# Shifted steps, later x loads and a longer estimate of a PSUM hold in a planned conv + ELU-MLP kernel

## Chip, cores and metric

One core of one Trainium2 chip. The metric is the device time of one execution in microseconds (us), lower is better. All runs named here are of one core and of the fast state; where a ratio to the kernel before is given, the two ran in turns on the same chip, and it is the mean time of one kernel's fast runs over the mean of the other's fast runs of the same rounds. It is therefore not quite the ratio of the medians that are quoted beside it. The experiments ran in four batches, on different chips (the record names 6, 13, 6 and 5), so absolute times of different batches are compared with less certainty.

## The reference

```python
def _attn_ref(x, weight):                       # x (8, 4096, 192), weight (8, 7)
    w = softmax(weight, axis=-1)                # cut: written out in numpy
    x_pad = np.concatenate([np.zeros((B, 6, D)), x], axis=1)
    idx = np.arange(S)[:, None] + np.arange(7)[None, :]
    x_unf = x_pad[:, idx, :].reshape(B, S, K, H, 24)
    return np.einsum('hk,bskhg->bshg', w, x_unf).reshape(B, S, D)

def _moe_ref(x, w_in, w_out):                   # x (32768, 192), w_in (192, 2048)
    h = x @ w_in
    g = np.where(h > 0.0, h, np.exp(np.minimum(h, 0.0)) - 1.0)
    return g @ w_out
```

A causal convolution of seven taps, one filter for each of 8 heads, is followed by a two-layer MLP with ELU between the layers.

## The kernel before

The 32768 rows go through in 32 blocks ("supers") of 1024. For each super TensorE computes

- four conv units (`"c"`, banded matrix times x),
- 16 pairs of h units (`"h"`: 128 of the 2048 hidden columns times 512 rows, one unit `r` for each half of the rows), three matmuls of 512 columns each,
- four output accumulators (`"o"` matmuls into a bank `"a"`), each open for eight pairs.

K is cut to 64, so that two matmuls run beside each other in the upper and the lower half of the array ("row half" 0 and 1; in the trace of this kernel a matmul of 64 x 512 and one of 64 x 192 both start at 209.06 us). An h unit goes through four engines: TensorE writes it to a PSUM bank, ScalarE (ACT) takes `E = exp(h)`, GpSimd (POOL) clamps E to 0..1, VectorE (DVE) computes `max(h, E - 1)` from E and the bank. Only then is the bank free. There are eight banks for h units, conv units and accumulators together, and a planner in Python fixes the whole order of TensorE, and which bank each unit takes, before the kernel is built:

```python
O_AT = (12, 15)              # pair at which the first and the second accumulator open
CONV_AT = (14, 18, 22, 25)   # pairs at which the conv units of a super two ahead run
HELD = {"h": 2500.0, "c": 1300.0, "a": 1400.0}   # ns from last matmul to a free bank, estimated
X_AT = ((1, 1, 1), (0, 1, 0))  # (conv unit, supers ahead, half): x load issued behind it

def take_bank(what):
    if what not in bank_of:
        b = min(range(NBANK), key=lambda b: freed[b])   # the bank expected free first
        bank_of[what], prior[what] = b, occupant[b]
        occupant[b], freed[b] = what, float("inf")

def h_items(n, r):
    def issue(j):
        take_bank(("h", n, r))
        plan.append((clock[r], ("h", n, r, j)))
        freed[bank_of["h", n, r]] = clock[r] + MM_H + HELD["h"] if j == 2 else float("inf")
# ... c_items, o_items and emit (which merges the two row halves by their clocks) are cut

# POOL: x loads stand between the clamps, issued by POOL (queue q0, software_dynamic, on the page)
for i, (n, u) in enumerate(units):
    # ... w_out load at pair W_OUT_AT = 5, zeroing of the pad rows: cut
    for to_load in x_before.get(i, ()):
        load_x(*to_load)
    W(s_exp, i + 1)
    g.tensor_scalar(out=E[:, i % NE, :], in0=E[:, i % NE, :],
                    scalar1=1.0, scalar2=0.0, op0=ALU.min, op1=ALU.max).then_inc(s_clp)

# TensorE: the first matmul into a bank waits for the last reader of its old user
def wait_bank(what):
    was = prior[what]
    # ...
    if was[0] == "h":   W(s_tt, tt_count(*was[1:]))       # DVE done
    elif was[0] == "c": conv_read(W, was[1])              # ACT done
    else:               W(s_oev[was[2]], was[1] + 1)      # ACT done
```

Below, "pair 5" means the pair with n mod 16 = 5 within a super (conv steps 14, 18, 22 and 25 are pairs 14, 2, 6 and 9), and "period" the time of one super.

## Time and profile before

| what | value | from |
|---|---|---|
| time | 754.69 us, median of 3 runs: 749.99, 754.69, 754.84 | the runs |
| span of the profiled run | 746.8 us (its time: 748.59) | page |
| TensorE, ACT, POOL, DVE busy | 99, 90, 89, 86% | page, part 1 |
| one period, measured | 22.21 us | trace: first h matmul of pair 32 to that of pair 464, over 27 |
| one period, as planned | 21.75 us | worked out in the prediction |

The lines behind these are in the prediction. One more view of the kernel before is needed later: the waits between 60 and 640 us, where the periods repeat. The columns are engine and line, who ended the wait, us in total, times, longest.

```profile
DVE gT L535 <- POOL E L455: 59.4, 150, 1.1
PEld H L589 <- DVE gT L535: 4.4, 26, 0.4
```

In 26 periods the weight load of conv unit 1 (line 589) waited for DVE, once each. This list sees only stretches in which the whole row PEld (TensorE's weight loads) is idle; a late matmul of one row half beside a busy other half isn't in it. That is why the prediction compares each start with the plan.

### The profile page before, as it was taken

To read this page: it belongs to the slowest core of one execution; us is meant where nothing else is said; L and a number is where in the kernel's file an instruction comes from. 1 tells how busy PE (TensorE), PEld (TensorE's weight loads), DVE (VectorE), ACT (ScalarE), POOL (GpSimd) and SP (SyncE) were. 2 spreads that over 40 slices of the span, in tenths; PEclk is the share of its full clock that TensorE was granted. 3 is DMA by queue.
4 is the path that set the end of the run, shared out by engine and by line. 5 is a ranking of instruction groups with operands and counts; after the bars stand their busy time and mean duration, and the time that the engine had idled before them with its cause. 6 is when DMAs were issued, how large, how long until landed. Compare 5 with 4: busy or idle time off the path is not lost.

```text
span 746.8 us, 27602 instructions
## 1 busy us (share of the span) xinstructions
PE 738.9 (99%) x11862; PEld 670.0 (90%) x11862; DVE 642.9 (86%) x1034; ACT 669.3 (90%) x1281; POOL 668.2 (89%) x1110
## 2 busy tenths in 40 slices
PE   8999999999999999999999999999999999999998
PEld 4379999999999999999999999999999999999997
DVE  2588898888998888889888989888899889898994
ACT  1689999999999999999999999999999999999993
POOL 3899999999999999999999999999999999998893
PEclk9999999999999999999999999999999999999999
DMA  5963455453445454445355345446344444453312
GB/s 99 135 87 70 77 86 80 76 84 71 89 74 89 66 83 75 90 70 94 60 86 90 72 72 92 68 87 84 70 81 84 83 72 83 71 94 69 56 46 66
DMA packets 135499, 59.32 MB, mean 79 GB/s; under 512 B 101680, under 2 KB 134576, under 8 KB 135376
## 3 DMA queue, kind: packets, MB, share of 16 engines
q0 software_dynamic: 44992, 17.67, 23.0%
q1 hardware_dynamic: 90112, 39.68, 22.9%
q8 instruction: 93, 1.52, 0.8%
q14 instruction: 30, 0.25, 0.1%
q10 hardware_dynamic: 272, 0.20, 0.1%
HBM read 34.80 MB, written 25.45 MB: 81 GB/s over the span
## 4 chain that ended last, share of the span: by engine, by line
PE 94%; DMA 3%; POOL 2%; DVE 1%; ACT 0%; issue 0%; SPq 0%
PE H L633 52%; PE H L610 37%; PE H L589 4%; POOL E L455 2%; DMA w_out<-in_moe_w_out_dram 1%; PE H L572 1%; DMA conv_band<-wprb 1%; POOL xg L405 1%; DMA wq<-in_weight_dram 0%; DMA Tk<-conv_band 0%; DVE gT L535 0%; ACT E L482 0%; ACT csb L478 0%; DVE osb L546 0%; DVE wprb L517 0%
## 5 line engine op out<-in xcount | busy, mean ns | idle before, releaser
L535 DVE SCALAR_TENSOR_TENSOR gT<-E,H 128x512 f16<-128x512 f32 x1024 | 637.2, 683 | 79.4 <-POOL E L455 78.7
L633 PE MATMUL H<-w_out,gT 64*128 64x192 f16 x8192 | 692.7, 243 | 1.6 <-DMA w_out<-in_moe_w_out_dram 1.4
L610 PE MATMUL H<-att,w_in 64*128 64x512 bf16 x3072 | 692.7, 376 | 0.5 <-DVE gT L535 0.3
L633 PEld LDWEIGHTS H<-w_out,gT 64*128 64x128 f16 x8192 | 622.5, 94 | 40.2 <-DVE gT L535 1.9
L455 POOL TENSOR_SCALAR E<-E 128x512 f32<-128x512 f32 x1024 | 604.6, 612 | 53.6 <-ACT E L482 39.3
L482 ACT ACTIVATE E<-H 128x512 f32<-128x512 f32 x1024 | 589.7, 603 | 52.9 <-PE H L610 26.4
L610 PEld LDWEIGHTS H<-att,w_in 64*128 64x128 bf16 x3072 | 273.8, 93 | 10.7 <-issue 5.1
L589 PE MATMUL H<-xg,Tm 64*112 64x240 bf16 x496 | 95.2, 272 | 0.1
L478 ACT ACTIVATE csb<-H 112x480 bf16<-112x480 f32 x126 | 70.9, 564 | 11.1 <-PE H L589 11.1
L491 ACT ACTIVATE osb<-H 128x384 f32<-128x384 f32 x127 | 62.7, 494 | 7.7 <-PE H L633 7.7
L405 POOL DMA_DIRECT2D xg<-in_x_dram x65 | 59.3, 912 | 6.0 <-DVE csb L525 5.8
L589 PEld LDWEIGHTS H<-xg,Tm 64*112 64x112 bf16 x496 | 53.9, 125 | 5.8 <-DVE gT L535 5.1
L572 PE MATMUL H<-zw 128*128 128x512 bf16 x86 | 24.6, 433 | 1.5 <-DVE zw L502 1.5
L572 PEld LDWEIGHTS H<-zw 128*128 128x128 bf16 x86 | 8.3, 109 | 15.3 <-issue 6.7
L525 DVE CAST csb<-H 112x480 bf16<-112x480 f32 x2 | 1.3, 658 | 10.4 <-PE H L589 10.4
L546 DVE COPY osb<-H 128x384 f32<-128x384 f32 x1 | 0.6, 557 | 7.9 <-PE H L633 7.9
L437 POOL DMA_DIRECT2D w_in<-w_in x1 | 0.7, 680 | 5.4 <-DMA w_in<-in_moe_w_in_dram 5.4
L423 POOL DMA_DIRECT2D w_in<-in_moe_w_in_dram x6 | 3.5, 599 | 0.9 <-DMA att<-csb 0.9
L589 PEld LDWEIGHTS H<-xg,Tk 64*112 64x112 bf16 (+1 forms) x16 | 2.6, 296 | 1.5 <-DMA Tk<-conv_band 1.5
L589 PE MATMUL H<-xg,Tk 64*112 64x240 bf16 (+1 forms) x16 | 2.9, 382 | 1.0 <-DMA Tk<-conv_band 1.0
L526 DVE COPY Tm<-Tk 118x896 bf16<-118x896 bf16 x1 | 2.2, 2190 | 0.0
L504 DVE TENSOR_REDUCE wmx<-wq 128x8 f32<-128x56 f32 x1 | 0.2, 210 | 2.2 <-DMA wq<-in_weight_dram 2.2
(17 smaller groups left out, 7.9 us busy)
## 6 DMA issues: line engine op xcount, KB each, us to landing
out_dram<-osb SPq DMA_DIRECT2D x127, 192.0 KB, 3.2
xg<-in_x_dram POOLq DMA_DIRECT2D x62, 240.0 KB, 5.0
w_in<-in_moe_w_in_dram POOLq DMA_DIRECT2D x6, 128.0 KB, 5.2
w_out<-in_moe_w_out_dram POOLq DMA_DIRECT2D x1, 768.0 KB, 8.6
att<-csb SPq DMA_TRANSPOSE x32, 3.8
xg<-in_x_dram POOLq DMA_DIRECT2D x2, 192.0 KB, 4.0
w_in<-w_in POOLq DMA_DIRECT2D x1, 384.0 KB, 4.4
w_in<-w_in SPq DMA_DIRECT2D x1, 384.0 KB, 6.6
```

The costliest lines, as they stand in the source:

```text
L405: g.dma_start(xg[0:rows, b, 2 * w0 + gr : 2 * w1 : 2, :], src).then_inc(s_x[b][gr], 16)
L423: g.dma_start(w_in[0:HP, j, c0:c1], bass.AP(tensor=moe_w_in.tensor, offset=8 * j * FF + c0, ap=[[CPH * FF, HEADS], [FF, 8], [1, c1 - c0]], ...
L455: g.tensor_scalar(out=E[:, i % NE, :], in0=E[:, i % NE, :], scalar1=1.0, scalar2=0.0, op0=ALU.min, op1=ALU.max,).then_inc(s_clp)
L478: a.activation(*conv_evac(W, m), ACT.Copy).then_inc(s_ce)
L482: a.activation(E[:, i % NE, :], H[:, bank_of[item], :], ACT.Exp).then_inc(s_exp)
L491: a.activation(osb[:, k % 2, g, :, :].rearrange("p k d -> p (k d)"), acc_of(k, g)[:, 0 : 2 * D], ACT.Copy,).then_inc(s_oev[g])
L526: v.tensor_copy(Tm[0:KW, :, :].rearrange("p h t -> p t h"), Tk[0:KW, :, :]).then_inc(s_tm)
L535: v.scalar_tensor_tensor(out=gT[:, s % NG3, q, u, :], in0=E[:, i % NE, :], scalar=1.0, in1=H[:, bank_of["h", n, u], :], op0=ALU.subtract, ...
L572: pe.matmul(H[:, bank_of[item[:2]], :], zw[:, 0:P], zw[:, 0:GS], start=True, stop=True)
L589: ins = pe.matmul(H[0:CW, bank_of["c", m], 256 * q : 256 * q + UC], Tm[rows, h, :] if s else Tk[rows, :, h], xg[rows, s % NXB, :, CPH * h ...
L610: ins = pe.matmul(H[:, bank_of[item[:3]], :], w_in[HP * r : HP * (r + 1), j, FC * q : FC * (q + 1)], att[HP * r : HP * (r + 1), s % 2, j, ...
L633: ins = pe.matmul(acc_of(k, g)[:, D * kb : D * (kb + 1)], gT[HP * rt : HP * (rt + 1), t % NG3, q, g, t0 : t0 + P], w_out[HP * rt : HP * (r ...
```

## The change

The intent, in the words given with it: the planned order is shifted, with conv units and x loads at other steps, the second accumulator one pair later, and banks picked by a longer estimate of an h unit's hold. The core of the diff:

```diff
-O_AT = (12, 15)
-CONV_AT = (14, 18, 22, 25)
+O_AT = (12, 16)
+CONV_AT = (14, 18, 23, 25)
-HELD = {"h": 2500.0, "c": 1300.0, "a": 1400.0}
+HELD = {"h": 2900.0, "c": 1300.0, "a": 1400.0}
-X_AT = ((1, 1, 1), (0, 1, 0))
+X_AT = ((2, 1, 1), (1, 1, 0))
+DVE_LAG = 1000.0
+E_DVE = ()
+X_WHOLE = False
+X_OFF = 0
```

The rest (cut) rewrites the loops of DVE and SyncE so that they follow a planned order too, and adds switches that are off here: evictions by DVE (`E_DVE` empty), one load for both halves (`X_WHOLE` false).

More of the change, by code (lines that the diff above doesn't have):

```diff
@@ L227, in bass_lightweight_conv__then__act_elu_kernel @@
     turn_at = {}
-    for item in pe_order:
+    dve_order, evacs, unit_at_conv = [], [], {}
+    for at, item in sorted(plan, key=lambda p: p[0]):
         if item[0] == "h" and item[3] == 2:
+            dve_order.append((at + DVE_LAG, item[:3]))
             unit_at[item[1:3]] = len(units)
@@ L234, in bass_lightweight_conv__then__act_elu_kernel @@
             act_order.append(item[:2])
+            unit_at_conv[item[1]] = at
         elif item[0] == "o" and item[-1]:
@@ L237, in bass_lightweight_conv__then__act_elu_kernel @@
             if turn_at[item[1:3]] == visits[item[1:3]]:
-                act_order.append(("e",) + item[1:3])
+                what = ("e",) + item[1:3]
+                if item[2] in E_DVE or item[1:3] == (NK - 1, 1):
+                    dve_order.append((at + AHEAD, what))
+                else:
+                    act_order.append(what)
+                evacs.append((at, what))
+    dve_order = [what for _, what in sorted(dve_order, key=lambda p: p[0])]
     assert len(units) == 2 * NP
@@ L250, in bass_lightweight_conv__then__act_elu_kernel @@
             if s + ahead < NS:
-                x_before.setdefault(before, []).append((s + ahead, gr))
+                x_before.setdefault(before + X_OFF, []).append((s + ahead, gr))
     x_before.setdefault(X_EARLY, []).append((2, 1))
@@ L298, in bass_lightweight_conv__then__act_elu_kernel @@
         s_cd = sema("s_cd")
-        s_od = sema("s_od")
         s_wdp = sema("s_wdp")
@@ L311, in bass_lightweight_conv__then__act_elu_kernel @@
         s_att = [sema(f"s_att{i}") for i in range(2)]
+        s_od = sema("s_od")
         s_cswap = sema("s_cswap")
@@ L330, in bass_lightweight_conv__then__act_elu_kernel, with x_whole @@
         WCOLS = ((0, P * QA), (P * QA, FF))
+        def x_whole(s):
+            return X_WHOLE and 2 < s < NS - 1
         x_need, z_need, z_count = {}, {}, 0
@@ L336, in bass_lightweight_conv__then__act_elu_kernel @@
             for g in range(2):
-                x_count[s % NXB][g] += 16 + 16 * ((s, g) in ((0, 0), (NS - 1, 1)))
+                if g == 0 or not x_whole(s):
+                    x_count[s % NXB][g] += 16 + 16 * ((s, g) in ((0, 0), (NS - 1, 1)))
                 x_need[s, g] = x_count[s % NXB][g]
@@ L372, in acc_of, with evacuated_by, out_evac @@
             return H[:, bank_of["a", k, g], :]
+        def evacuated_by(W, k, g):
+            on_dve = [item[1:] for item in dve_order if item[0] == "e"]
+            if (k, g) in on_dve:
+                W(s_od, on_dve.index((k, g)) + 1)
+            else:
+                W(s_oev[g], [a for a in act_order if a[0] == "e" and a[2] == g].index(("e", k, g)) + 1)
+        def out_evac(W, k, g):
+            W(s_out[k % 2], 32 * (k // 2))
+            W(s_fin[g], k + 1)
+            return (
+                osb[:, k % 2, g, :, :].rearrange("p k d -> p (k d)"),
+                acc_of(k, g)[:, 0 : 2 * D],
+            )
         def transpose(eng, W, s):
@@ L397, in load_x @@
                     ).then_inc(s_x[0][0], 16)
+                if x_whole(s):
+                    if gr == 0:
+                        src = bass.AP(
+                            tensor=x_flat.tensor,
+                            offset=(s * SUP - PAD) * D,
+                            ap=[[D, P], [CW * D, NWIN], [GS * D, 2], [1, D]],
+                        )
+                        g.dma_start(
+                            xg[:, b, :, :].rearrange("p (w g) d -> p w g d", g=2), src
+                        ).then_inc(s_x[b][0], 16)
+                    return
                 def windows(w0, w1, rows):
@@ L485, in _scalar @@
                 else:
-                    _, k, g = item
-                    if (k, g) == (NK - 1, 1):
-                        continue
-                    W(s_fin[g], k + 1)
-                    W(s_out[k % 2], 32 * (k // 2))
-                    a.activation(
-                        osb[:, k % 2, g, :, :].rearrange("p k d -> p (k d)"),
-                        acc_of(k, g)[:, 0 : 2 * D],
-                        ACT.Copy,
-                    ).then_inc(s_oev[g])
-            W(s_od, 1)
+                    a.activation(*out_evac(W, *item[1:]), ACT.Copy).then_inc(s_oev[item[2]])
+            evacuated_by(W, NK - 1, 1)
             out_group(a, NK - 1, 1)
@@ L528, in _vector @@
             ).then_inc(s_tm)
-            for i, (n, u) in enumerate(units):
+            for item in dve_order:
+                if item[0] == "e":
+                    v.tensor_copy(*out_evac(W, *item[1:])).then_inc(s_od)
+                    continue
+                _, n, u = item
+                i = unit_at[n, u]
                 s, q = divmod(n, NQ)
@@ L538, in _vector @@
                     scalar=1.0,
-                    in1=H[:, bank_of["h", n, u], :],
+                    in1=H[:, bank_of[item], :],
                     op0=ALU.subtract,
@@ L542, in _vector @@
                 ).then_inc(s_tt)
-            b = (NK - 1) % 2
-            W(s_fin[1], NK)
-            W(s_out[b], 32 * (NS - 1))
-            v.tensor_copy(
-                osb[:, b, 1, :, :].rearrange("p k d -> p (k d)"),
-                acc_of(NK - 1, 1)[:, 0 : 2 * D],
-            ).then_inc(s_od)
         @block.tensor
@@ L563, in wait_bank @@
                 else:
-                    W(s_oev[was[2]], was[1] + 1)
+                    evacuated_by(W, *was[1:])
             turns, done = {0: 0, 1: 0}, {}
@@ L671, in _sync @@
             ).then_inc(s_band, 16)
-            for item in act_order:
+            sync_work = []
+            for m in range(CU - 1, CU * NS, CU):
+                sync_work.append((unit_at_conv[m], ("c", m)))
+            sync_work += [(at, item) for at, item in evacs]
+            for _, item in sorted(sync_work):
                 if item[0] == "c":
-                    s, u = divmod(item[1], CU)
-                    if u == CU - 1:
-                        transpose(sy, W, s)
+                    transpose(sy, W, item[1] // CU)
                     if item[1] == CU - 1:
@@ L681, in _sync @@
                         sy.dma_start(w_in[HP:P, :, c0:c1], w_in[0:HP, :, c0:c1]).then_inc(s_wd, 16)
-                elif item[0] == "e" and item[1:] != (NK - 1, 1):
-                    W(s_oev[item[2]], item[1] + 1)
+                elif item[1:] != (NK - 1, 1):
+                    evacuated_by(W, *item[1:])
                     out_group(sy, *item[1:])
```

## The prediction

> **What bounds the kernel now.** I read the page first: its busy shares, its chain, its costliest groups.
>
> ```profile
> PE 738.9 (99%) x11862; PEld 670.0 (90%) x11862; DVE 642.9 (86%) x1034; ACT 669.3 (90%) x1281; POOL 668.2 (89%) x1110
> PE 94%; DMA 3%; POOL 2%; DVE 1%; ACT 0%; issue 0%; SPq 0%
> L535 DVE SCALAR_TENSOR_TENSOR gT<-E,H 128x512 f16<-128x512 f32 x1024 | 637.2, 683 | 79.4 <-POOL E L455 78.7
> L405 POOL DMA_DIRECT2D xg<-in_x_dram x65 | 59.3, 912 | 6.0 <-DVE csb L525 5.8
> ```
>
> TensorE sets the end, but "99% busy" cannot tell whether it runs at full pace: two 64-row halves of the array work beside each other, and one half hides the other's gap. So I worked out what a period must cost. A period is one block of 1024 rows, 16 "pairs" of h units; the trace spaces matmuls of one half 216 ns apart (512 columns) and 82.5 ns (192), and the plan has 102.5 for 240. One half does 48 x 216 + 128 x 82.5 + 8 x 102.5 ns = **21.75 us**. Then I looked for the real period in the order in time of POOL (first of two answers) and DVE (second), near the middle of the run.
>
> ```profile
> 199.87 1.33 POOL L455 TENSOR_SCALAR E<-E 128x512 f32<-128x512 f32 x2
> 201.14 0.89 POOL L405 DMA_DIRECT2D xg<-in_x_dram  x1
> 202.07 4.70 POOL L455 TENSOR_SCALAR E<-E 128x512 f32<-128x512 f32 x8
> 206.71 0.90 POOL L405 DMA_DIRECT2D xg<-in_x_dram  x1
> ...
> 223.33 0.90 POOL L405 DMA_DIRECT2D xg<-in_x_dram  x1
> ```
>
> ```profile
> 202.73 4.89 DVE L535 SCALAR_TENSOR_TENSOR gT<-E,H 128x512 f16<-128x512 f32 x8 [0.81 <-POOL E L455]
> 208.31 4.92 DVE L535 SCALAR_TENSOR_TENSOR gT<-E,H 128x512 f16<-128x512 f32 x8 [0.69 <-POOL E L455]
> ```
>
> The same x load is issued at 201.14 and at 223.33, so the period is **22.2 us**: 0.45 us over the plan, 32 times. The reader is to see how each POOL issue of 0.9 us leaves DVE idle 0.7 to 0.8 us and then with a queue of eight units. Third, the order in time around two late TensorE starts.
>
> ```profile
> 204.67 0.12 PEld L589 LDWEIGHTS H<-xg,Tm 64*112 64x112 bf16 x1 [0.15 <-DVE gT L535]
> 204.67 0.31 PE L589 MATMUL H<-xg,Tm 64*112 64x240 bf16 x1
> ...
> 209.06 0.39 PE L610 MATMUL H<-att,w_in 64*128 64x512 bf16 x1
> ```
>
> The conv matmul at 204.67 takes the PSUM bank of an h unit that DVE frees as the third of the queue begun at 202.73 (202.73 + 2 x 0.60 + 0.68 = 204.61). The h matmul at 209.06 takes a bank freed by the first unit of the queue begun at 208.31 (ends 208.99). Both start 0.06 us after the release, and every period repeats them. By comparing each start with the planned time, the first late start is worth 0.20 us on its half (and 0.04 as its next weight load is late too), the second 0.21 us on the other half, and a third, conv unit 2, 0.04. The chain calls all this PE, since the other half was busy meanwhile.
>
> [...]
>
> **The change part by part.** No arithmetic is added or removed: the counts of instructions per engine are the same in both built programs, X_WHOLE is off, E_DVE empty, and DVE's order is unchanged. Only the order moves. The rule for each hand-over of a bank: wait = hold + 0.06 us - distance, with the hold from the old user's last matmul start to the end of its last reader, and the distance from that start to the planned start of the new user. From the trace, per place in the period: h holds are 2.42 to 2.75 us where POOL is undisturbed and 2.77 to 3.10 in the six to eight units behind an x issue; a conv unit holds 1.15 us. The planner of the kernel, followed item by item, gives the distances.
>
> Before: x issues fall at pairs 14 and 2 of the period. Conv unit 1 (pair 2) takes the bank of the r = 0 unit of pair 15, distance 2.83, hold 2.99: wait 0.22. The h unit of pair 5 takes that of pair 2, distance 2.83, hold 2.99: wait 0.22. The trace has 0.20 and 0.21, so the rule works.
>
> 1. *x loads one conv unit later* (X_AT): issues move from pairs 14 and 2 to pairs 2 and 7. This clears the long holds at pairs 14 to 1 (they fall to about 2.45 to 2.6), so conv unit 1 has 2.83 against 2.5: its wait goes, -0.24. In exchange pairs 7 to 9 get holds of about 3.0. The data still come in time: issue to landing is 5.0 us (6.4 at most in the view of that line), the conv that needs them is 7 pairs, 9.5 us, later.
> 2. *HELD h 2.5 to 2.9*: the planner now gives the h units of pairs 5 to 7 banks with a distance of 3.49 us, against holds of up to 3.03: the second wait goes, -0.21. It shifts the squeeze to conv banks and accumulators.
> 3. *Conv unit 2 at pair 7, second accumulator at 16*: conv unit 2 takes the bank of pair 4's unit, distance 2.83 against 2.77 + 0.06: about 0, as tight as can be. The second accumulator's odd turn (pair 8) takes conv unit 2's bank, distance 1.09 to 1.15 against 1.15 + 0.06: **a new wait of 0.06 to 0.11**, plus 0.05 where the next half waits for its turn. The pair-10 unit takes that of pair 7: 3.15 against 3.03 + 0.06, just clear.
>
> Sum per period: 0.45 - 0.24 - 0.21 - 0.04 + 0.10 + 0.05 (rounding up for the tight ones) = 0.11 to 0.16 left; I take 0.16, a gain of 0.29. Steady periods: about 29, as the first two and the end differ: 29 x 0.29 = 8.4 us. Against it: about 0.4 us at the start, where the longer estimate makes early units wait for conv banks (most of it hidden, since TensorE then waits for w_out anyway), and 0.3 us at the tail, where the plan itself ends 697.75 instead of 697.42 us. Net **-7.7 us, an estimate**.
>
> **The rivals.** (a) *The wait only moves*: the backlog behind an x issue now meets conv unit 2, pair 10 and the odd accumulator with 0.0 to 0.1 us to spare. For it: h holds of r = 0 vary by 0.1 between neighbouring places. Against it: most distances grew from 2.83 to 3.49. If two of the three lose 0.15 more, the gain is 0.29 - 0.2 = 0.1 a period, some 3 us: about 751. (b) *All waits vanish*: 0.40 a period, 12 us, about 742 from the median. (c) *The bound is elsewhere* (ACT, POOL, DVE at 86 to 90%): then nothing moves, 754; against it, each of the three has idle time behind TensorE and the two waits are seen. (d) *Later x loads come too late* for conv or for the zeroing on POOL (7 times): some us slower; the landing of 6.4 us against 8 to 9.5 speaks against it.
>
> **Range and chances.** Before ran at 749.99, 754.69 and 754.84, and 748.59 under the profile: two levels 5 us apart. A POOL issue 0.08 us longer would do that (2 x 0.08 x 30 = 4.8 us, an estimate from the two waits with no slack), but this is not shown; it may as well lie in the start. The change should take off 7.7 from either level: 747 or 742. I put the middle at **745.5 us**, range 739 to 751.5. To be faster by over 2% of the 753 mean it would have to save 15 us, more than all steady waits together (0.45 x 32 = 14.4): 0.05. Slower by over 2%: 0.02. Within 2%: 0.93.
>
> **What would show each step right or wrong.** In the changed trace: the spacing of the x issues from period to period (21.9 us right; 22.1 or more wrong); conv unit 1 and pair 5 without a wait for DVE; TensorE's repeated wait now before the second accumulator, released by ACT's conv eviction, near 0.1 us; DVE's idle of 0.7 to 0.8 us behind POOL at pairs 2 and 7. The prediction fails if a hand-over with under 0.1 us to spare waits in each period, if POOL's issues last longer beside other transfers, or if the start differs.

## The result, and the profile after

The first comparison, four runs each: the changed kernel 740.92 us (740.60 to 742.02), the kernel before 752.34 us (749.52 to 754.84), ratio 0.9852 with a 95% interval of 0.9804 to 0.9900. By the 2% rule that is "same"; the interval lies clear of 1. Compared again with 6 and 27 runs (below) the ratio was 0.9866.

The page of the changed kernel, with the lines that answer to those of before:

```profile
span 738.9 us, 27599 instructions
PE 730.6 (99%) x11859; PEld 686.2 (93%) x11862; DVE 639.3 (87%) x1034; ACT 674.9 (91%) x1281; POOL 670.1 (91%) x1110
PE 94%; DMA 3%; POOL 2%; DVE 0%; ACT 0%; issue 0%; DVEq 0%; SPq 0%
L575 DVE SCALAR_TENSOR_TENSOR gT<-E,H 128x512 f16<-128x512 f32 x1024 | 633.6, 683 | 73.8 <-POOL E L499 72.2
L449 POOL DMA_DIRECT2D xg<-in_x_dram x65 | 59.3, 912 | 6.5 <-DVE csb L560 6.3
```

The busy shares and the chain look as before: the work is the same and TensorE was "99% busy" in both. Only the weight-load row moves, from 670 to 686 us at the same number of loads, whose lengths add up to 1130 and 1132 us, so fewer of them lie beside each other; I did not follow that further. The page alone would not tell what was gained.

The order in time does. First POOL, then DVE, in the changed kernel near 200 us (start, length, what):

```profile
205.19 0.89 POOL L449 DMA_DIRECT2D xg<-in_x_dram  x1
206.11 5.89 POOL L499 TENSOR_SCALAR E<-E 128x512 f32<-128x512 f32 x10
211.95 0.90 POOL L449 DMA_DIRECT2D xg<-in_x_dram  x1
212.89 4.86 POOL L499 TENSOR_SCALAR E<-E 128x512 f32<-128x512 f32 x8
...
227.06 0.90 POOL L449 DMA_DIRECT2D xg<-in_x_dram  x1
```

```profile
206.77 6.07 DVE L575 SCALAR_TENSOR_TENSOR gT<-E,H 128x512 f16<-128x512 f32 x10 [0.69 <-POOL E L499]
213.55 4.92 DVE L575 SCALAR_TENSOR_TENSOR gT<-E,H 128x512 f16<-128x512 f32 x8 [0.71 <-POOL E L499]
```

The same x load comes at 205.19 and 227.06: a period of **21.87 us** here, 21.89 over 27 periods, where it was 22.21. The two issues still cost DVE 0.7 us of idleness each and leave it with a queue of eight to ten units. So the disturbance is not gone. What changed is who stands behind it: in the waits between 60 and 640 us, the 26 waits of the conv unit's weight load have become one.

```profile
DVE gT L575 <- POOL E L499: 55.6, 126, 1.0
PEld H L622 <- DVE gT L575: 0.3, 1, 0.3
```

The remaining 0.14 us per period can be placed by the order in time around conv unit 2 and the second accumulator of the changed kernel:

```profile
209.17 1.28 DVE L575 SCALAR_TENSOR_TENSOR gT<-E,H 128x512 f16<-128x512 f32 x2
209.91 0.31 PE L622 MATMUL H<-xg,Tm 64*112 64x240 bf16 x1
```

```profile
211.21 0.56 ACT L522 ACTIVATE csb<-H 112x480 bf16<-112x480 f32 x1
211.84 0.10 PEld L666 LDWEIGHTS H<-w_out,gT 64*128 64x128 f16 x1
```

Conv unit 2 takes the bank of pair 4's unit: the first of the two units begun at 209.17 ends near 209.85 (0.68 us), and the conv matmul starts at 209.91, 0.04 us later than the plan has it (0.05 in the mean of the periods), with 0.04 more because its next weight load is late. The second accumulator takes the bank of that conv unit: ACT's eviction ends at 211.77, the accumulator's weights load at 211.84, another 0.04 us late, and 0.01 with its next matmul. These four add up to the 0.14. Both are hand-overs that the prediction had named as the tight ones. The pair-10 unit also starts 57 ns after its release and is 0.05 us late, but on the row half that is the less late of the two, so that nothing is added.

### The profile page after: what moved, and what is told of

Its sections match the earlier page's. It is cut to its first block, busy times and chain, and to the rows that moved or that the text cites. A ratio compares the mean times of both kernels' runs of the same rounds, so it can differ in the third digit from the quotient of the medians.

```text
span 738.9 us, 27599 instructions
## 1 busy us (share of the span) xinstructions
PE 730.6 (99%) x11859; PEld 686.2 (93%) x11862; DVE 639.3 (87%) x1034; ACT 674.9 (91%) x1281; POOL 670.1 (91%) x1110
## 4 chain that ended last, share of the span: by engine, by line
PE 94%; DMA 3%; POOL 2%; DVE 0%; ACT 0%; issue 0%; DVEq 0%; SPq 0%
PE H L666 53%; PE H L643 36%; PE H L622 3%; POOL E L499 2%; DMA w_out<-in_moe_w_out_dram 1%; PE H L605 1%; DMA conv_band<-wprb 1%; POOL xg L449 1%; DMA Tk<-conv_band 0%; DMA wq<-in_weight_dram 0%; ACT E L526 0%; DVE gT L575 0%; DVE osb L566 0%; DVE wprb L552 0%; ACT osb L530 0%
## 5 line engine op out<-in xcount | busy, mean ns | idle before, releaser
L643 PE MATMUL H<-att,w_in 64*128 64x512 bf16 x3072 | 680.0, 377 | 0.6 <-ACT csb L522 0.5
L666 PE MATMUL H<-w_out,gT 64*128 64x192 f16 x8192 | 679.9, 243 | 0.7 <-DMA w_out<-in_moe_w_out_dram 0.5
L622 PE MATMUL H<-xg,Tm 64*112 64x240 bf16 x496 | 92.5, 266 | 0.6 <-ACT csb L522 0.6
L522 ACT ACTIVATE csb<-H 112x480 bf16<-112x480 f32 x126 | 70.9, 564 | 11.9 <-PE H L622 11.9
L622 PEld LDWEIGHTS H<-xg,Tm 64*112 64x112 bf16 x496 | 57.5, 126 | 3.6 <-ACT csb L522 0.9
L560 DVE CAST csb<-H 112x480 bf16<-112x480 f32 x2 | 1.3, 658 | 11.2 <-PE H L622 11.2
```

Of the source, the lines that this page charges most:

```text
L522: a.activation(*conv_evac(W, m), ACT.Copy).then_inc(s_ce)
L622: ins = pe.matmul(H[0:CW, bank_of["c", m], 256 * q : 256 * q + UC], Tm[rows, h, :] if s else Tk[rows, :, h], xg[rows, s % NXB, :, CPH * h ...
L643: ins = pe.matmul(H[:, bank_of[item[:3]], :], w_in[HP * r : HP * (r + 1), j, FC * q : FC * (q + 1)], att[HP * r : HP * (r + 1), s % 2, j, ...
L666: ins = pe.matmul(acc_of(k, g)[:, D * kb : D * (kb + 1)], gT[HP * rt : HP * (rt + 1), t % NG3, q, g, t0 : t0 + P], w_out[HP * rt : HP * (r ...
```

## The experiments

Every profiled run gives the period without noise (it repeats to within 0.01 us), while the time of a run scatters by some 5 us. So the table gives both. "Loss" is the period less the planned 21.75 us. "From the period" is what the period's difference from before makes of the ratio over 29 periods, an estimate against the mean of before, 752 us; the ratio is the measured one. Where a wait of a single unit is given below, it is what its late start adds to the lateness of the later of the two row halves against the plan, in the mean of 26 periods; the waits of a period then add up to its loss.

| run | loss per period, us | expected by the hand-over rule | from the period | measured ratio (95%) | runs |
|---|---|---|---|---|---|
| before | 0.46 | - | 1 | 1 | - |
| code_only | 0.46 | as before | 1.000 | 1.0004 (0.9988-1.0020) | 20 |
| x_only | 0.57 | 0.56 to 0.6 | 1.004 | 1.0044 (1.0015-1.0073) | 9 |
| steps_only | 0.62 | 0.62 to 0.67 | 1.006 | 1.0074 (1.0047-1.0100) | 6 |
| held_only | 0.35 | 0.25 to 0.3 | 0.996 | 0.9943 (0.9924-0.9961) | 14 |
| no_x | 0.24 | 0.25 to 0.3 | 0.991 | 0.9890 (0.9864-0.9916) | 4 |
| no_held | 0.42 | 0.41 to 0.47 | 0.998 | 0.9992 (0.9973-1.0011) | 12 |
| no_steps | 0.46 | 0.44 to 0.5 | 1.000 | 0.9993 (0.9975-1.0010) | 12 |
| after_again (whole change) | 0.14 | 0.11 to 0.16 | 0.988 | 0.9866 (0.9836-0.9897) | 6 |
| pool_pad | 0.82 | 0.9 | 1.014 | 1.0131 (1.0092-1.0169) | 4 |
| w_early | 0.14 | 0.14 | 0.987 | 0.9846 (0.9813-0.9879) | 6 |
| best_plan | 0.07 | 0 to 0.1 | 0.985 | 0.9840 (0.9804-0.9876) | 6 |
| best_both | 0.06 | 0.07 | 0.985 | 0.9827 (0.9795-0.9859) | 6 |

The two theories of the first seven: **joint hand-overs** (the prediction's rule, worked through the whole plan: HELD and the steps move the distances of all later units, since a bank is picked by what the others do, and X_AT, which moves no matmul and no bank, moves the long holds to other units) against **parts that add up** (each part of the change takes away its own wait). The kernels of these seven are the changed kernel's file with some of its constants set back; with the whole change they are all eight combinations of three parts (x loads, steps, hold). The rule was worked by a small program that follows the plan item by item with the durations of the trace of before; its figures are estimates, and they are on record with each run.

### One part at a time

**code_only**: all four constants as before.

```diff
-O_AT = (12, 16); CONV_AT = (14, 18, 23, 25); HELD h 2900.0; X_AT = ((2, 1, 1), (1, 1, 0))
+O_AT = (12, 15); CONV_AT = (14, 18, 22, 25); HELD h 2500.0; X_AT = ((1, 1, 1), (0, 1, 0))
```

> The changed code with all four constants as before. Both theories: it is the kernel before in all but line numbers and the order of waits on the queue of the SyncE: period of the x issues 22.20 us, the waits of conv unit 1 and of the h unit of pair 5 as before, time within 0.3% of the kernel before. If the rewritten order of the output queue matters, the time moves here.

Measured: period 22.21 us, ratio 1.0004. The rewritten loops change nothing that these runs show; all of the gain is in four constants.

**x_only**: before, with the x loads later.

```diff
-X_AT = ((1, 1, 1), (0, 1, 0))
+X_AT = ((2, 1, 1), (1, 1, 0))
```

> The kernel before with the x loads one conv unit later, nothing else. Theory of joint hand-overs (wait = hold + 0.06 us - distance, worked through the whole plan): the backlog now meets conv unit 3 at pair 9 (about 0.37 us) while the wait at pair 5 stays: 0.56 to 0.6 us lost per period, SLOWER than before by about 4.5 us. Rival, parts add up: it takes away the 0.24 us wait of conv unit 1 and leaves the rest, 0.21 lost per period, faster by about 7 us.

Measured: 754.68 us (750.83 to 758.58), ratio 1.0044, loss 0.57. Conv unit 1 no longer waits, as the prediction said of this part. But conv unit 3 now waits 0.29 us and 0.04 with its next weight load (it takes the bank of pair 6's unit, whose hold is 3.15 us, against 2.59 in the kernel before), and pair 5 still waits its 0.22. In the waits between 60 and 640 us a conv unit still waits once a period, 7.2 us in all where it was 4.4 before:

```profile
PEld H L622 <- DVE gT L575: 7.2, 26, 0.3
```

The part that the prediction credited with 0.24 us per period makes the kernel slower when it comes alone: the wait is not taken away, it goes to another unit. "Parts that add up" falls here.

**steps_only**: before, with conv unit 2 and the second accumulator moved.

```diff
-O_AT = (12, 15)
-CONV_AT = (14, 18, 22, 25)
+O_AT = (12, 16)
+CONV_AT = (14, 18, 23, 25)
```

> The kernel before with conv unit 2 at pair 7 and the second accumulator one pair later, nothing else. Joint hand-overs: 0.62 to 0.67 us lost per period (waits at the h units of pairs 1 and 5, 0.27 each, and at conv units), slower than before by about 6 us. Rival, parts add up: no part of the two known waits is touched, so 22.20 us a period and the same time.

Measured: 756.57 us (755.01 to 758.97), ratio 1.0074, loss 0.62. The h units of pairs 1 and 5 wait 0.25 and 0.29 us each, as expected by the joint rule. In the waits between 60 and 640 us, the weight loads that waited are now those of h units (line 643), and 51 of them:

```profile
PEld H L643 <- DVE gT L575: 11.3, 51, 0.4
```

**held_only**: before, with the hold of an h unit estimated at 2.9 us.

```diff
-HELD = {"h": 2500.0, "c": 1300.0, "a": 1400.0}
+HELD = {"h": 2900.0, "c": 1300.0, "a": 1400.0}
```

> The kernel before with the hold of an h unit estimated at 2.9 in place of 2.5 us, nothing else. Joint hand-overs: waits of 0.10 at conv unit 2, 0.06 at the second accumulator and turns, 0.25 to 0.3 us lost per period, faster than before by 3.5 us. Rival, parts add up: the wait of pair 5 goes, 0.24 lost, faster by 6 us; these two hardly differ in time, so the place of the wait decides: joint says conv unit 1 does not wait any more although the x loads have not moved, the rival says it still waits 0.20 us.

Measured: 747.21 us (744.74 to 751.06), ratio 0.9943, loss 0.35. In the main a hit for the joint rule: pair 5 no longer waits, conv unit 2 waits 0.10 + 0.04, the accumulators 0.03 each time. But I had written that conv unit 1 would not wait at all, and it does, by 0.06 + 0.04 us instead of 0.2: that is a miss by 0.1 us per period, about the precision of the rule.

### One part taken out

**no_x**, **no_held** and **no_steps** are the whole change with one part set back.

```diff
 no_x:      -X_AT = ((2, 1, 1), (1, 1, 0))   +X_AT = ((1, 1, 1), (0, 1, 0))
 no_held:   -"h": 2900.0                     +"h": 2500.0
 no_steps:  -O_AT = (12, 16), CONV_AT[2] = 23   +O_AT = (12, 15), CONV_AT[2] = 22
```

> All of the change but the later x loads. Joint hand-overs: 0.25 to 0.3 us lost per period (conv unit 1 waits 0.10, the odd second accumulator 0.06, turns), as with the longer hold alone; faster than before by about 3.5 us, slower than the whole change by about 5. Rival, x loads are what pays: no gain or loss against before.

> All of the change but the hold of 2.9. Joint hand-overs: 0.41 to 0.47 us lost per period, the h unit of pair 5 waiting 0.27 as before; the same time as before within 0.3%. Rival, the gain is spread over the parts: 0.2 to 0.3 lost, some 4 us faster.

> All of the change but the moved steps (conv unit 2 stays at pair 6, the second accumulator at 15). Joint hand-overs: 0.44 to 0.5 us lost per period, conv unit 3 waiting 0.15 and conv unit 2 0.10; the same time as before within 0.4%. Rival, the steps are neutral: 0.11 to 0.16 lost, as with the whole change, 8 to 11 us faster.

Measured: no_x 743.95 us, ratio 0.9890, loss 0.24; no_held 751.65 us, ratio 0.9992, loss 0.42; no_steps 751.01 us, ratio 0.9993, loss 0.46. All three losses lie at what the joint rule gave (no_x 0.01 below its range). The time that I had put beside it for no_x, 3.5 us faster than before, was a miss: the ratio gives 8 us, the period about 6.6 (29 x 0.226). Without the later x loads two thirds of the gain stay (0.23 of 0.32 us). Without the longer estimate, or without the moved steps, it is all but gone, though neither of these does much or any good alone: steps alone lose 0.16, the estimate alone gains 0.11, both together (no_x) gain 0.23. The waits between 60 and 640 us of no_steps show what the whole change lacks: two conv units (line 622) wait in every period.

```profile
PEld H L622 <- DVE gT L575: 11.0, 52, 0.4
```

### Is it POOL's queue that makes the waits?

**pool_pad**: before, with a memset of 6 x 192 elements behind each x load.

```diff
+        pad = sbuf("pad", [PAD, 2 * NS, D], BF16)
+        pads = iter(range(2 * NS))
                 for to_load in x_before.get(i, ()):
                     load_x(*to_load)
+                    g.memset(pad[:, next(pads), :], 0.0)
```

> The kernel before with one small memset (6 x 192, 0.22 to 0.25 us on GpSimd, its own buffer each) behind each x load. If the backlog behind the x issues is what sets the two waits, each of them grows by the memset: 0.45 + 2 x 0.22 = about 0.9 us lost per period, some 13 us slower (ratio 1.017), although POOL is busy only 2% more and TensorE stays the bound by its busy share. Rival, POOL's delay is hidden as its busy share of 89% suggests: the same time within 0.3%.

Measured: 762.98 us (759.63 to 763.45), ratio 1.0131, loss 0.82. The page of this run (busy, chain, the memsets), its order in time on POOL, and its waits between 60 and 640 us (L592 is the conv line, L613 that of h):

```profile
PE 748.0 (98%) x11862; PEld 672.2 (88%) x11862; DVE 644.0 (85%) x1034; ACT 669.8 (88%) x1281; POOL 683.4 (90%) x1170
PE 59%; POOL 32%; DVE 3%; DMA 3%; ACT 2%; issue 1%; SPq 0%
L456 POOL MEMSET pad<- 6x192 bf16 x60 | 14.9, 248 | 0.1
208.09 0.89 POOL L407 DMA_DIRECT2D xg<-in_x_dram  x1
208.97 0.25 POOL L456 MEMSET pad<- 6x192 bf16 x1
PEld H L592 <- DVE gT L538: 8.7, 25, 0.5
PEld H L613 <- DVE gT L538: 7.4, 25, 0.3
```

Fifteen microseconds of tiny memsets, on an engine that is 90% busy and not the bound, cost 10 us of a kernel whose TensorE is 98% busy. The two waits of a period grew by 0.36 us together, against 0.44 expected (twice 0.22), as the holds of the two units whose banks are waited for grew by 0.18 each (2.99 to 3.17): the direction and most of the size. The chain of the page, which had 2% on POOL before, now has 32% there. This shows that the hold of the units behind an x issue sets the two waits. It also means that a busy share says nothing of these places: at the hand-overs without slack POOL is on the path.

### The two levels of the kernel before

The 3 runs of the kernel before had two levels 5 us apart, and the prediction left open where they lie. More runs make a range of the upper one: of the 40 that ran with code_only, 15 took 749.3 to 750.8 us and 25 took 751.7 to 754.8. The profiles caught both ends. The windows from 36 to 48 us of the kernel before, then of code_only, which has the same plan, in a run of the upper level. Of the 5.1 us between their spans, 1.2 lie before the first h matmul, 3.4 in pairs 0 to 16 and 0.4 after pair 480. The columns: window, its length, busy us (instructions) of TensorE, weight loads, DVE, ACT and POOL, then granted clock, DMA share, GB/s.

```profile
40.00:44.00 4.00, 2.67 (x37) 2.08 (x39) 3.42 (x6) 2.70 (x6) 3.03 (x6) 1.00 0.61 92
44.00:48.00 4.00, 3.90 (x65) 3.67 (x63) 3.22 (x7) 3.83 (x8) 3.93 (x7) 1.00 0.14 14
```

```profile
40.00:44.00 4.00, 1.07 (x8) 0.21 (x6) 4.00 (x7) 1.99 (x4) 3.07 (x6) 1.00 1.39 129
44.00:48.00 4.00, 3.56 (x27) 2.68 (x29) 0.88 (x3) 1.20 (x3) 1.22 (x2) 0.57 0.24 51
```

In code_only TensorE is busy for 1.07 of 4 us before 44, and then the granted clock is 0.57, and 27 matmuls are done where the kernel before did 65. What it waited for is the only load of w_out; waits between 36 and 48 us of code_only:

```profile
PEld H L666 <- DVE gT L575: 3.8, 1, 3.8
PE H L666 <- DMA w_out<-in_moe_w_out_dram: 3.3, 1, 3.3
```

Over the profiles of kernels that load w_out at pair 5 (first h matmul to the first of pair 16):

| run | w_out, issue to landing, us | half clock after 40 us | pairs 0 to 16, us |
|---|---|---|---|
| before, x_only, steps_only, after | 8.6 to 8.9 | none | 23.8 to 24.0 |
| best_plan | 8.2 | none | 23.9 |
| no_x | 10.3 | none | 25.4 |
| code_only, held_only, after_again, no_held | 10.4 to 10.8 | 3.4 us | 27.0 to 27.4 |
| no_steps, pool_pad | 11.9, 11.2 | 6.8 us | 29.3, 29.2 |

So the upper level goes with a late landing of w_out, by 1.7 to 3.3 us, plus (mostly) one window of 3.4 us at half clock that follows the gap (granted clock 0.57 in code_only and 0.58 in after_again between 44 and 48 us; 1.00 in the kernel before). It does not come from the change. Why w_out lands late in some runs stays open. **after_again** asked whether the changed kernel has that level too.

> The changed kernel again, for its spread. The profiles so far say that the two levels of the kernel before come from the first load of w_out: where it lands 10.5 us after its issue and not 8.6, TensorE idles about 3 us before the first output matmul and one clock window of 3.4 us runs at half clock. If so, the changed kernel has an upper level too, 3 to 5 us above 741, in some of its runs, and the ratio comes near 0.987. Rival: the changed kernel has lost the upper level (its four runs lie within 1.4 us), and the ratio stays 0.985.

Measured: 742.40 us (739.27 to 745.62), 6 runs, ratio 0.9866 to 27 runs of before at 752.31 us. Its profiled run is one of the upper level. So the changed kernel has the upper level too, and the first four runs, all within 1.4 us, missed it, it seems by chance. 0.9866, of more runs, is the better figure, and it is near what the period gives (0.988).

**w_early**: the changed kernel with w_out loaded behind pair 1.

```diff
-W_OUT_AT = 5
+W_OUT_AT = 1
```

> The changed kernel with the load of w_out issued behind the first pair and not the fifth. If the late landing of w_out (8.6 us or 10.3 to 11.9) makes the two levels, TensorE no longer waits for w_out, no half-clock window falls near 44 us, and the upper level goes: runs within 2 us of each other, mean 1 to 3 us below the changed kernel's (about 740, ratio 0.983). Rival, the spread comes from elsewhere at the start: the same spread of 6 us and the same mean. The loss per period stays at 0.14.

Measured: 741.27 us (738.51 to 742.09), ratio 0.9846, loss 0.14. In its profile w_out lands 10.5 us after its issue, TensorE does not wait for it, and no half clock follows. The spread is 3.6 us in place of 6.4, five of six runs within 1.1 us (one run too many for the 2 us expected); but the mean, 741.0, is not clearly below after_again's 742.6, which was taken on another chip, and the first four runs of the changed kernel had 741.1. The cause of the upper level is supported, the gain in the mean is inconclusive. Some scatter remains that lies before the first h unit: it starts at 22.2 to 25.0 us in the 14 profiles (24.6 to 25.0 in the five where the half clock between 14 and 22 us lasts 6.8 us, but also 24.9 in after_again, where it lasts 3.4).

### A plan picked by the rule

**best_plan**: the rule worked over some thousands of settings of the same constants; the one taken has no wait by the rule.

```diff
-O_AT = (12, 16)
-CONV_AT = (14, 18, 23, 25)
-HELD = {"h": 2900.0, "c": 1300.0, "a": 1400.0}
-X_AT = ((2, 1, 1), (1, 1, 0))
+O_AT = (12, 15)
+CONV_AT = (13, 18, 24, 26)
+HELD = {"h": 3000.0, "c": 1500.0, "a": 1400.0}
+X_AT = ((1, 1, 1), (0, 1, 0))
```

> A plan picked by the hand-over rule: conv units at pairs 13, 18, 24 and 26, second accumulator at 15, x loads behind units 0 and 1 as in the kernel before, holds of 3.0, 1.5 and 1.4 us. The rule gives 0.0 us lost per period, at most 0.1 with the holds 0.08 longer than in the sheet: 1.5 to 4 us faster than the changed kernel (ratio to before about 0.983). Rival, the margins under 0.1 us do not hold and a wait of 0.1 to 0.2 comes back: no better than the changed kernel.

Measured: 740.13 us (736.72 to 743.64), ratio 0.9840, period 21.82, loss 0.07. The loss is half of the changed kernel's, with the x loads where the kernel before had them: by the period the expectation is a hit. In time, 0.9840 against 0.9866 for the changed kernel, the intervals overlap. One hand-over is still at the edge: conv unit 1 starts 55 ns after the release, with a hold of 2.81 us.

**best_both**: this plan and the early w_out.

> The plan of the last run and the early load of w_out together. If the two act in different stages, the loss per period is 0.07 as with the plan alone and TensorE does not wait for w_out: mean about 738.5, ratio to before about 0.981, faster than the changed kernel by 3 to 4 us; spread smaller than the 7 us of the plan alone, but not below 3, since the start before the first h unit (22.2 to 25.0 us in the profiles) stays. Rival, they collide in the start (w_out beside the x loads): no better than the plan alone.

Measured: 738.70 us (737.68 to 740.06), ratio 0.9827, loss 0.06; the windows of its profile show TensorE busy 3.80 to 4.00 of 4 us from 36 us on. It has the lowest ratio and, of the versions with six runs, the smallest spread, 2.4 us (I had expected no less than 3). Whether it is over 2% faster than before is unclear, as the interval takes in 0.98. In time, its lead over best_plan (738.8 against 740.4 in the mean, on another chip) is within the intervals; the lead over the changed kernel rests on a period 0.08 us shorter, 2.2 us in 29, and on the start.

## Why the prediction was right or wrong

- **The bound and the place of the loss: right.** The period was 0.46 us over plan because units behind an x issue freed their banks late. Setting the constants back (code_only) brings the loss back exactly, and lengthening POOL's disturbance (pool_pad) lengthens it.
- **The sum per period: right, its make-up in part by luck.** Left per period: 0.11 to 0.16 predicted, 0.14 measured; period 21.9 predicted, 21.89 measured. The new wait at the second accumulator, the squeeze at conv unit 2 and the edge at pair 10 all stood where they were said to stand. But the prediction put all that is left on the accumulator (0.06 to 0.11, and 0.05 for a turn) and "about 0" on conv unit 2; measured are 0.05 at the accumulator and 0.05 + 0.04 at conv unit 2. The "- 0.04" for conv unit 2 was not part of the 0.45 either: its wait lay on the less late half, and conv unit 1 (0.18 + 0.04) and pair 5 (0.22 + 0.01) make up the loss alone. These errors cancel. Pair 10's distance is 3.04 us in the plan, not 3.15, so it was not "just clear"; that it costs nothing is due to the other half.
- **How the sum is shared out: wrong.** The step "x loads one conv unit later ... its wait goes, -0.24" gives the x loads a gain of their own. On their own they lose 0.11 (x_only), and the rest of the change has two thirds of the gain without them (no_x). The wait of conv unit 1 does go, but the working priced only what the move clears. "In exchange pairs 7 to 9 get holds of about 3.0" was left without a price, as it was held against the distances of the finished plan; in the plan of before the second x load falls at pair 6, whose unit hands its bank to conv unit 3 (distance 2.83), which then waits 0.33. And with HELD and the steps moved, conv unit 1's wait falls to 0.11 + 0.04 even with the old x loads. The three parts work as one plan, and a list "part by part" with a sign for each can't be right even where its sum is.
- **The size in time: low by 1 us in the traces, the rest is scatter.** Predicted -7.7 us; the ratios give -11.1 (0.9852, interval 7.5 to 14.7) and -10.1 us (0.9866, 7.7 to 12.3), so that -7.7 lies at the edge of the noise. The profiles of before and after, both with an early w_out, say more: from the first h matmul to the end it took 723.6 and 714.8 us, 8.8 less. Term by term: "29 x 0.29 = 8.4" is 29 x 0.32 = 9.4 (pairs 16 to 480: 644.64 and 635.25 us), the "about 0.4 us at the start" was 0.04 (pairs 0 to 16: 23.76 and 23.80), the "0.3 us at the tail" was 0.5 (from pair 480: 55.19 and 55.72). What the ratios have over 8.8, 1.3 to 2.3 us, is within the scatter of the start.
- **The two levels: the guess was wrong, and marked as not shown.** A POOL issue 0.08 us longer is not what happens: code_only's period in an upper-level run is the same 22.21. What goes with the upper level is the landing of w_out (10.5 us after its issue in code_only, 8.6 in the kernel before) and a window of 3.4 us at half clock after it. The middle of 745.5 us, 753 less 7.7, did not hang on it. Measured medians of 740.9 and 742.4 lie within the range.
- **Rivals.** (a), the wait only moves, came true to a small part: three hand-overs now start 55 to 57 ns after the release, and two of them make the 0.14 that is left. ("Most distances grew from 2.83 to 3.49", said against it, is too much: the bank of pair 2's unit is taken at 3.49 now, but conv units 0 to 2 keep 2.83.) (b), all waits vanish, put the time at 742, which is where it came out; only the 0.14 us left in the period refutes it. By the time alone (b) would have looked right. (c) is refuted by the times, (d) by the waits between 60 and 640 us, where no wait of TensorE for an x load stands.

## What to carry to other kernels

Where a plan hands few buffers round many users, work each hand-over as hold plus signal minus distance, with holds measured behind each disturbance and not a single average; then change the plan as a whole, since a constant that alone makes it slower can be needed for the gain. A busy share of 99% on one engine does not clear the others (here 0.46 of 22.21 us per period were lost beside it): compare the measured period with the planned one, and test a suspected engine by adding a little work to it at the suspected place. Judge small gains by the period in the trace, which repeats to 0.01 us, before the run time, which here scatters by 5 us for reasons that lie mostly in the first 50 us.

## What the traces show besides

- The matmuls of the two row halves do not all start in program order. In the kernel before, the h matmul of the other half that stands behind the first two matmuls of the late conv unit 1 and two output matmuls in the program starts at 204.72 us, ahead of the second conv matmul (204.82) and of both output matmuls (204.92 and 205.00). Over the whole trace 2330 of 11861 neighbours in program order have the later one recorded as starting earlier; this count is an estimate, since a record doesn't name its half and was given to the one whose order and spacing it fits. Only starts were compared; ends are modelled in this profile.
- What an x load of 240 KB costs the work queued behind its issue on GpSimd: 0.9 us for the issue, a hold longer by about 0.6 us for the first unit behind it (pair 6's: 2.59 us in before, 3.15 in x_only, where an issue stands ahead of it), and a queue on VectorE of eight to ten units.
- The number of buffers stays at eight, and the order, with the choice of which one each unit takes, is worth 0.39 of 22.2 us per period (best_plan against before, x loads behind the same conv units).
